# A transformer block on one core: VectorE copies the accumulator, maxima in another order, and two more blocks in seven products

## The chip, the core and the metric

The kernel runs on one core of a Trainium2 chip. The core has a matrix engine (TensorE, PE in the profile; PEld is its loading of weights), a vector engine (VectorE, DVE), an engine for functions (ScalarE, ACT), a general one (GpSimd, POOL), and a queue (SyncE, SP) that here only issues transfers (DMAs) between the chip's memory and the on-chip buffer, SBUF. TensorE writes to eight banks in a small memory of its own, PSUM; a bank holds 128 x 512 numbers of 32 bits. The metric is the device time of one execution, in microseconds (us).

## The reference

One block of a transformer in 32-bit floats: layer norm, attention of 32 heads of width 20, and a gated feed-forward part, each with its residual.

```python
B, S, D, H = 1, 2048, 640, 32
B, S, D, F = 1, 2048, 640, 1728
...
qkv = (x @ wqkv).reshape(B, S, 3, H, Dh)
scores = jnp.einsum("bhqd,bhkd->bhqk", q, k) * (Dh ** -0.5)
p = _softmax(scores, axis=-1)
o = jnp.einsum("bhqk,bhkd->bhqd", p, v)
return o.transpose(0, 2, 1, 3).reshape(B, S, D) @ wo
...
g = _silu(x @ w_gate)
u = x @ w_up
return (g * u) @ w_down
...
h = x + _A_ref(_layernorm(x, axis=-1), A_wqkv, A_wo)
h2 = h + _B_ref(_layernorm(h, axis=-1), B_w_gate, B_w_up, B_w_down)
```

## The kernel before

Each engine runs its own instructions in the order in which the program issues them; a manual schedule fixes that order, and tiles with few buffers make one engine wait for another. Numbers are kept exact by splitting a matrix into a high and a low part, so that one product takes three matmuls.

**Projections**, to about 350 us: queries, keys and values for all heads, and the first row maxima of the scores.

**Attention**, about 350 to 1450 us. The work is cut into 32 units: `u` counts groups of four heads times four chunks of 512 queries. A unit has 16 steps, `kt`, one for each 128 keys. In a step TensorE weighs the values of the step two before (`W`: `weigh`, four matmuls at once, one per head, into the tile `acc`, in records of L1319), and makes four products of scores (`s` for two heads, `S` for the other two, which lie in other rows of the array; L1309), each of which ScalarE turns into probabilities with one exponential (L1315). Between them stand three products whose row maxima VectorE takes for a later unit (`m` and `M`, L274 and L280; `next_max`). A string of letters in `ORDER` gives the order of one step; even and odd steps have one each. Scores rotate through four PSUM banks, maxima through three, and `acc` has the eighth: the next unit's first `W` can't begin until `acc` has been copied out. That copy is made in `row_sums` (L1329): it is issued in step 1 of the next unit, behind the last `W` of the unit, on ScalarE. Its transfers, a reciprocal in step 4 and a multiplication in step 9 follow.

When all maxima of a unit are there (`full`), VectorE joins them into one negative maximum per row (`max_all`, a reduction of 128 x 64), GpSimd splits it (`max_parts`), four steps later VectorE turns it (`max_turn`), and two steps after that it is loaded beside the queries (`max_load`).

In the same steps, one task per step, weights are prepared for the feed-forward part: `prepare_weights` leaves split blocks of the down weights in `d_d` (plain) and, for two blocks together, seven combinations in `j_d`.

**Feed-forward**, about 1500 us to the end. Tokens are taken in two halves (`pair` 0 and 1), and the 1728 hidden columns in 14 blocks `f`: the loop goes over 28 elements, `ELEMENTS`, in the order of blocks 13, 0, 1 to 12, once for each half. An element makes its gate and up products (`blocks`, L1492) in eight steps. After the products of a step, `step()` issues some down products that have become ready, taken from the queue `waiting` by `next_down`; how many per element is a number in `RATES`, spread evenly over its steps. VectorE adds the parts of gate and up (L1709), multiplies them to the hidden values `y` (L1713), and adds each down product to a sum.

A down group is 256 tokens (`tp` 0 to 3 in a half) against one block of the hidden columns (`plain`: four products of 3 matmuls, 320 columns wide, added to the result `h` by L1592) or two blocks (`seven`: seven products in place of eight, after Strassen and Winograd; three of them go to `h`, four to sums of their own, `own`, L1610). GpSimd and ScalarE prepare the operands, `yp`. After the last group in seven products the four sums are joined to `h` by eight additions (`put_together`, L1625), which are put in a list, `chores`, and issued on GpSimd, two in each `step()`. In the first half the blocks 2 to 11 go in seven products, in the second half the blocks 0 to 9; there blocks 10, 11, 12 and 13 are plain. Down products use four PSUM banks, gate and up four others. When the loop is over, the rest of `waiting` is issued, and the result of each 128 tokens is stored as soon as its last addition, that of block 12, is made (L1651).

Of the kernel before, what the change touches and what calls it, by code (L numbers as in the profile page):

```python
# [11 lines left out]
F32R = mybir.dt.float32r  # L12
# [26 lines left out]
GD = G * DH  # L39

ORDER = ("WsSmmSsM", "WSsMMsSm")


@with_exitstack
def tile_block(ctx: ExitStack, tc: tile.TileContext, x, wqkv, wo, wg, wu, wd, out):
# [15 lines left out]
    t_d = [dram.tile([P, 8 * CH], F32R, name=f"t_d{i}") for i in range(2)]  # L61
    w_d = [dram.tile([P, 8, 4 * P], F32R, name=f"w_d{f}") for f in range(NF)]
    d_d = {
        f: dram.tile([P, 2, 2 * HALF], F32R, name=f"d_d{f}") for f in (0, 1, *range(NF - 4, NF))
    }
    j_d = [dram.tile([P, 7, 2 * HALF], F32R, name=f"j_d{j}") for j in range((NF - 2) // 2)]
    h_d = dram.tile([2, P, TPC, D], F32, name="h_d")
# [216 lines left out]
    def max_all(u):  # L284

        ends[u] = stk.tile([P, G * TPC], F32, name="neg", tag="neg", bufs=2)
        nc.vector.tensor_reduce(  # L287
            ends[u], mxs[u].rearrange("p b h t k -> p (b h t) k"), axis=AX.X, op=ALU.max, negate=True
        )

    def max_parts(u):

        neg = ends[u]
        both = ends[u] = stk.tile([P, 2, G * TPC], F32R, name="neg2", bufs=2)
        nc.gpsimd.tensor_copy(both[:, 0], neg)  # L295
        nc.gpsimd.tensor_tensor(
            out=both[:, 1], in0=neg, in1=both[:, 0].bitcast(F32), op=ALU.subtract
        )

    def max_turn(u):  # L300

        turned = stk.tile([P, 2 * G * TPC], F32, name="turned", bufs=2)
        nc.vector.transpose(turned, ends.pop(u).bitcast(F32).rearrange("p i n -> p (i n)"))
        nc.sync.dma_start(m_d[u % 2], turned)

    def max_load(u):

        n = 2 * TPC
        rows = m_d[u % 2].rearrange("(q i r) c -> i r q c", q=4, i=2)
        for b in range(2):  # L310
            for i in range(2):
                row = b * ROW + NPART + i
                dst = queries[u][row : row + 1].bitcast(F32).rearrange("r j c -> r (j c)")
                nc.sync.dma_start(dst, rows[i, b * n : (b + 1) * n])

    def max_finish(u):

        m = (ps_one if u else ps_max)()[: G * TPC, :P]
        nc.tensor.transpose(m, ends.pop(u), ident)
        parts = stk.tile([G * TPC, 2, P], F32R, name="m2", tag="m2", bufs=1)  # L320
        split(m, parts[:, 0], parts[:, 1], nc.vector)
        for b in range(2):
            for i in range(2):
                row = b * ROW + NPART + i
                first = b * 2 * TPC
                nc.sync.dma_start(
                    queries[u][row : row + 1].bitcast(F32).rearrange(
                        "r j (t p) -> r (j t) p", t=TPC
                    ),
                    parts[first : first + 2 * TPC, i, :].bitcast(F32),  # L330
                )
# [994 lines left out]

    def row_sums(acc, *queues):
        o = pc.tile([P, CH], F32, name="o", bufs=2)
        nc.scalar.activation(o, acc, AF.Copy)  # L1329
        r = pc.tile([P, 16], F32, name="r")  # L1330
        for j in range(G):
            queues[j % len(queues)].dma_start(
                r[32 * j : 32 * j + 32, :],
                o[32 * j + DH : 32 * j + DH + 1, :].rearrange("r (p f) -> r p f", p=32),
            )
        return o, r
# [47 lines left out]
    for u in range(NU):  # L1384
# [9 lines left out]
        for kt in range(NT):  # L1394
            now[0] = u * NT + kt
            probs = [pp.tile([P, 2, CH], F32, name="probs") for _ in range(2)]
            heads = [[0, 2], [1, 3]]
            order = ORDER[now[0] % 2] if singles[0] or singles[1] else "WsSsS"
            for op in order:
                if op in "mM":  # L1400
                    next_max(int(op == "M"))
# [14 lines left out]
                        last_ring.fill()  # L1416
            todo.append((u, kt, probs))
            for v in full:
                max_all(v)
                if v in (1, NU - 1):  # L1420
                    later.setdefault(now[0] + 2, []).append(lambda v=v: max_finish(v))
                else:
                    max_parts(v)
                    later.setdefault(now[0] + 4, []).append(lambda v=v: max_turn(v))
                    later.setdefault(now[0] + 6, []).append(lambda v=v: max_load(v))
            full.clear()
            if kt == 0 and u + 3 < NU:
                load_queries(u + 3)
# [107 lines left out]

    def own(pair, f):

        return f >= NF - 4 if pair else f < 2 or f >= NF - 2

    SLOTS = ("A11", "A12", "A22", "S1", "S2", "S3", "S4")
    sums, chores, stored = {}, [], []
# [2 lines left out]
    class Group:  # L1545
# [68 lines left out]
        def put_together(self):  # L1614

            h = h_c[self.c]
            at = [h[:, self.t + i, k * HALF : (k + 1) * HALF] for i in range(2) for k in range(2)]
            one, six, seven, five = sums[self.tp]
            for out, x in (
                (at[0], one), (six, one), (at[1], six), (at[1], five), (seven, six),  # L1620
                (at[2], seven), (five, seven), (at[3], five),
            ):
                chores.append((
                    self.pair, self.tp,
                    lambda o=out, x=x: nc.gpsimd.tensor_tensor(out=o, in0=o, in1=x, op=ALU.add),  # L1625
                ))
# [33 lines left out]
    def next_down():  # L1660
        if not waiting:
            return
        g = waiting[0]
        prepare_some()
        f, i = g.steps.pop(0)
        f(i)
        if not g.steps:
            waiting.pop(0)
# [246 lines left out]
    def spread_over(n, steps, first=0):  # L1915
# [3 lines left out]
    RATES = {  # L1919
# [3 lines left out]
    }  # L1923
    again = []

# [78 lines left out]
        before = ys  # L2004
    while waiting:
        next_down()


_INS = ["A_x", "A_wqkv", "A_wo", "B_w_gate", "B_w_up", "B_w_down"]
# [26 lines left out]
```

## Time and profile before

| | |
|---|---|
| Median of 3 runs | 2009.06 us (2008.3 to 2011.39) |
| The profiled execution's own time | 2007.79 us |
| Its span in the trace | 2006.0 us |
| Busy: PE, DVE, ACT, POOL | 1997.4, 1602.9, 1434.6, 799.9 us |
| Exponentials (ACT L1315) | 2048, 613 ns each |
| Row maxima (DVE L280) | 1472, 684 ns each |
| Copies of the accumulator (ACT L1329) | 32, 629 ns each |

Times are counted from the start of the span; the execution is 1.8 us longer than its span. An engine takes the next instruction before the last one has ended, so the distance from one start to the next is less than the duration of one: it is called the pitch below. A busy PE is not PE at its peak, since the ends of matmuls are modelled: whether it lost time is read from the distances between starts.

### The profile page before, as it was taken

Reading aid. Unit: us, or ns where it says so; the run is one execution under the profiler, and the core shown is the slowest. Engines: PE = TensorE matmul, PEld = TensorE weight load, DVE = VectorE, ACT = ScalarE, POOL = GpSimd, SP = SyncE. Lnnn points to the kernel's source line nnn. Section 1 sums busy time; section 2 is a strip of 40 time slices with the busy share of each in tenths; the row PEclk is TensorE's granted clock in tenths of the full one; section 3 lists DMA queues with packets and bytes.
Section 4 is the critical chain, followed back from the end, with each engine's and each line's share of the span. In section 5 each row is a group of like instructions: output and inputs, shape, how many; then the busy total and the mean of one; then the engine's idle time right before and its main releaser. Section 6 shows DMA issues by size and latency. Waiting matters only on the chain.

```text
span 2006.0 us, 40039 instructions
## 1 busy us (share of the span) xinstructions
PE 1997.4 (100%) x14346; PEld 1246.5 (62%) x14346; DVE 1602.9 (80%) x2806; ACT 1434.6 (72%) x2811; POOL 799.9 (40%) x1206
## 2 busy tenths in 40 slices
PE   9999999999999999999999999999999999999999
PEld 8999995333333333333333333345598888888888
DVE  5778778898898888988988888886387766676677
ACT  4777778999999999999999999987633222212221
POOL 7564423344343443443500020011156444854555
PEclk9999999999999999999999999999999999999999
DMA  7887573442634534435412132221158654974542
GB/s 250 263 260 260 182 216 83 129 145 92 188 107 136 159 126 144 160 117 181 153 50 78 28 90 55 81 63 61 50 193 300 229 178 162 357 265 159 205 151 94
DMA packets 201541, 310.98 MB, mean 155 GB/s; under 512 B 55960, under 2 KB 89816, under 8 KB 200320
## 3 DMA queue, kind: packets, MB, share of 16 engines
q1 hardware_dynamic: 194752, 284.83, 43.5%
q0 software_dynamic: 6496, 23.60, 4.0%
q8 instruction: 114, 1.87, 0.4%
q14 instruction: 83, 0.68, 0.1%
q10 hardware_dynamic: 96, 0.00, 0.0%
HBM read 208.73 MB, written 99.32 MB: 154 GB/s over the span
## 4 chain that ended last, share of the span: by engine, by line
PE 99%; DVE 0%; ACT 0%; issue 0%; POOL 0%; POOLq 0%; DVEq 0%; ACTq 0%
PE acc L1319 25%; PE ps_a L1492 17%; PE ps_one L1309 16%; PE ps_max L274 13%; PE ps_one L647 10%; PE ps_b L1587 9%; PE ps_max L239 3%; PE ps_max L1037 2%; PE ps_b L1037 2%; PE ps_two L809 0%; PE ps_two L700 0%; PE ps_max L1072 0%; ACT ps_max L251 0%; PE ps_a L1858 0%; PE ps_max L573 0%
## 5 line engine op out<-in xcount | busy, mean ns | idle before, releaser
L1315 ACT ACTIVATE probs<-ps_one 128x512 f32<-128x512 f32 x2048 | 1055.9, 613 | 55.4 <-PE ps_one L1309 29.8
L280 DVE TENSOR_REDUCE mx<-ps_max 128x1 f32<-128x512 f32 x1472 | 924.9, 684 | 106.2 <-PE ps_one L1309 77.6
L1309 PE MATMUL ps_one<-q_stk,k_stk 62*128 62x512 f32 x2048 | 579.7, 448 | 0.3 <-ACT probs L1315 0.3
L1319 PE MATMUL acc<-probs,v_stk 128*32 128x512 f32 x4096 | 546.3, 604 | 0.0
L1309 PEld LDWEIGHTS ps_one<-q_stk,k_stk 62*128 62x128 f32 x2048 | 247.5, 184 | 444.7 <-ACT probs L1315 424.9
L274 PE MATMUL ps_max<-k_stk,q_stk 60*128 60x512 f32 x1472 | 373.5, 426 | 0.1
L274 PEld LDWEIGHTS ps_max<-k_stk,q_stk 60*128 60x128 f32 x1472 | 272.6, 186 | 26.7 <-DVE mx L280 1.3
L1709 DVE TENSOR_TENSOR tmp<-ps_a,tmp 128x512 f32<-128x512 f32 x208 | 141.2, 689 | 121.0 <-PE ps_a L1492 93.0
L261 DVE TENSOR_REDUCE mx<-ps_max 128x2 f32<-128x512 f32 x288 | 180.7, 684 | 60.2 <-PE ps_max L239 55.7
L1319 PEld LDWEIGHTS acc<-probs,v_stk 128*32 128x32 f32 x4096 | 80.9, 108 | 180.0 <-issue 167.8
L251 ACT ACTIVATE ps_max<-ps_max 128x512 f32<-128x512 f32 x288 | 151.8, 583 | 39.6 <-PE ps_max L239 38.2
L1587 PE MATMUL ps_b<-halves,yp 128*128 128x320 f32 x1032 | 178.7, 308 | 0.2 <-DVE h L1592 0.2
L1587 PEld LDWEIGHTS ps_b<-halves,yp 128*128 128x128 f32 x1032 | 165.2, 188 | 16.0 <-DVE h L1592 0.5
L1492 PE MATMUL ps_a<-t,units 128*128 128x512 f32 x624 | 162.5, 396 | 0.0
L1354 POOL TENSOR_TENSOR o<-o,rb 128x512 f32<-128x512 f32 x31 | 39.9, 1288 | 269.3 <-DMA q_stk<-m_d 146.5
L90 POOL TENSOR_TENSOR yp<-y,yp 128x256 fp32r<-128x256 f32 x96 | 60.4, 629 | 186.9 <-ACT yp L89 179.0
L1492 PE MATMUL ps_a<-z,units 128*128 128x512 f32 x516 | 133.9, 394 | 0.0
L1492 PEld LDWEIGHTS ps_a<-t,units 128*128 128x128 f32 x624 | 112.6, 188 | 18.5
L295 POOL CAST neg<-neg 128x16 fp32r<-128x16 f32 x30 | 5.9, 198 | 281.2 <-DVE neg L287 281.2
L1592 DVE TENSOR_TENSOR h<-ps_b,h 128x320 f32<-128x320 f32 x248 | 109.8, 480 | 5.8 <-PE ps_b L1587 4.3
L647 PE MATMUL ps_one<-z_hi,w_lo 64*128 64x512 f32 x380 | 111.8, 392 | 0.0
L647 PE MATMUL ps_one<-z_hi,w_hi 64*128 64x512 f32 x380 | 111.5, 393 | 0.0
(220 smaller groups left out, 2748.4 us busy)
## 6 DMA issues: line engine op xcount, KB each, us to landing
units<-w_d SPq DMA_DIRECT2D x186, 256.0 KB
w_d<-stage SPq DMA_DIRECT2D x106, 256.0 KB
halves<-j_d SPq DMA_DIRECT2D x70, 320.0 KB
j_d<-stage SPq DMA_DIRECT2D x42, 320.0 KB
raw<-k_d SPq DMA_DIRECT2D x64, 160.0 KB
k_stk<-k_d SPq DMA_DIRECT2D x64, 160.0 KB
q_stk<-q_d SPq DMA_DIRECT2D x64, 160.0 KB
raw<-q_d SPq DMA_DIRECT2D x54, 160.0 KB
```

What stands on the lines that cost most here:

```text
L251: nc.scalar.activation(ps, ps, AF.Relu)
L261: nc.vector.tensor_reduce(mx[:, b, :, t, kc], ps.rearrange("p (j n) -> p j n", j=2), axis=AX.X, op=ALU.max,)
L274: nc.tensor.matmul(ps, queries[u][rows, pair, t * P : (t + 1) * P], keys[u // NC][rows, pair, kc * CH : (kc + 1) * CH], start=True, stop=True,
L280: nc.vector.tensor_reduce(mxs[u][:, b, pair, t, kc : kc + 1], ps, axis=AX.X, op=ALU.max)
L647: nc.tensor.matmul(ps, a[rows], b[rows], start=(i == n == 0), stop=(i == 1 and n == last), skip_group_check=True,)
L1309: nc.tensor.matmul(ps, keys[u // NC][rows, p, kt * P : (kt + 1) * P], queries[u][rows, p, :], start=True, stop=True,)
L1315: nc.scalar.activation(probs[p][:, b, :], ps, AF.Exp, scale=scale)
L1319: nc.tensor.matmul(acc[32 * j : 32 * j + 32, :], values[u // NC][:, kt, j * VW : j * VW + 32], probs[j // 2][:, j % 2, :], start=(kt == 0) ...
L1492: nc.tensor.matmul(ps.rearrange("p (t n) -> p t n", t=TPC), w[k][:, i], z[k][:, :, j], start=(first and m == 0), stop=(last and m == len(n ...
L1587: nc.tensor.matmul(ps, a, b, start=(n == 0), stop=(n == len(pairs) - 1))
L1592: nc.vector.tensor_tensor(out=h, in0=ps, in1=h, op=ALU.add)
L1709: add = lambda out, ps, x: nc.vector.tensor_tensor(out=out, in0=ps, in1=x, op=ALU.add)
```

## The change

It has four parts. The copy of `acc` in `row_sums` goes from ScalarE to VectorE, in all units but the last. The first five steps of each unit but the first take their order from a new table, `BEGIN`. Where the maxima of a unit become complete in step 15, they are joined four steps later, and turned and loaded four steps later too. In the second half of the feed-forward part, blocks 10 and 11 go through the seven products; the joining of the sums therefore comes after them, just ahead of block 12. For the last two groups of tokens (`tp` 2 and 3) its eight additions are made at once on VectorE, and not put into the list for GpSimd. `RATES` of the last three elements are 16, 15 and 30 in place of 18, 22 and 26, and in the rest of `waiting` one of the list's additions is issued after each product.

```diff
+BEGIN = (
+    "WmSmsSMs", "WsSmSsMM", "WSsMMsmS", "WsMSmsSm", "WmSmsSsM",
+)
...
-        f: dram.tile([P, 2, 2 * HALF], F32R, name=f"d_d{f}") for f in (0, 1, *range(NF - 4, NF))
+        f: dram.tile([P, 2, 2 * HALF], F32R, name=f"d_d{f}") for f in (0, 1, *range(NF - 2, NF))
...
-        nc.scalar.activation(o, acc, AF.Copy)
+        if len(queues) == 1:
+            nc.vector.tensor_copy(o, acc)
+        else:
+            nc.scalar.activation(o, acc, AF.Copy)
...
-            order = ORDER[now[0] % 2] if singles[0] or singles[1] else "WsSsS"
+            order = BEGIN[kt] if u and kt < len(BEGIN) else ORDER[kt % 2]
+            if not (singles[0] or singles[1]):
+                order = "WsSsS"
...
-                max_all(v)
+                at = now[0]
                 if v in (1, NU - 1):
-                    later.setdefault(now[0] + 2, []).append(lambda v=v: max_finish(v))
+                    max_all(v)
+                    later.setdefault(at + 2, []).append(lambda v=v: max_finish(v))
                 else:
-                    max_parts(v)
-                    later.setdefault(now[0] + 4, []).append(lambda v=v: max_turn(v))
-                    later.setdefault(now[0] + 6, []).append(lambda v=v: max_load(v))
+                    if kt == NT - 1:
+                        at += 4
+                        later.setdefault(at, []).append(lambda v=v: (max_all(v), max_parts(v)))
+                    else:
+                        max_all(v)
+                        max_parts(v)
+                    later.setdefault(at + 4, []).append(lambda v=v: max_turn(v))
+                    later.setdefault(at + 6, []).append(lambda v=v: max_load(v))
...
-        return f >= NF - 4 if pair else f < 2 or f >= NF - 2
+        return f >= NF - 2 if pair else f < 2 or f >= NF - 2
...
+                if (self.pair, self.tp // 2) == (1, 1):
+                    nc.vector.tensor_tensor(out=out, in0=out, in1=x, op=ALU.add)
+                    continue
...
-        25: (18, 0), 26: (22, 0), 27: (26, 0),
+        25: (16, 0), 26: (15, 0), 27: (30, 0),
...
     while waiting:
         next_down()
+        if chores:
+            chores.pop(0)[2]()
```

On VectorE, at the start of a unit whose maxima became complete in step 15, before the change: `neg` is the joining, `turned` the turning, and each `mx` a row maximum of 128 x 512.

```order
L287 TENSOR_REDUCE neg<-mx_9492 128x16
L280 TENSOR_REDUCE mx_10182<-ps_max 128x1 x9
L303 STREAM_TRANSPOSE turned<-neg_10163 128x32
L280 TENSOR_REDUCE mx_10182<-ps_max 128x1 x6
L1340 RECIPROCAL r<-r 128x16
```

The same place after it:

```order
L283 TENSOR_REDUCE mx_10169<-ps_max 128x1 x3
L1333 COPY o<-acc 128x512
L283 TENSOR_REDUCE mx_10169<-ps_max 128x1 x6
L290 TENSOR_REDUCE neg<-mx_9490 128x16
L283 TENSOR_REDUCE mx_10169<-ps_max 128x1 x6
L1346 RECIPROCAL r<-r 128x16
L283 TENSOR_REDUCE mx_10169<-ps_max 128x1 x6
L306 STREAM_TRANSPOSE turned<-neg_10271 128x32
```

The copy stands behind the three maxima of step 0 and ahead of those of step 1; the joining has gone from the unit's first place to behind the maxima of step 2.

On TensorE, steps 0 and 1 of a unit before the change, from the last `W` but one of the unit before (`acc`) to its last:

```order
L1319 MATMUL acc<-probs,v_stk_5637 32x512 x4
L1309 MATMUL ps_one<-q_stk,k_stk_125 128x512 x2
L274 MATMUL ps_max<-k_stk_125,q_stk 128x512 x2
L1309 MATMUL ps_one<-q_stk,k_stk_125 128x512 x2
L274 MATMUL ps_max<-k_stk_125,q_stk 128x512
L1319 MATMUL acc<-probs,v_stk_5637 32x512 x4
```

The same place after it, and the products behind the last `W`:

```order
L1322 MATMUL acc<-probs,v_stk_5635 32x512 x4
L277 MATMUL ps_max<-k_stk_123,q_stk 128x512
L1312 MATMUL ps_one<-q_stk,k_stk_123 128x512
L277 MATMUL ps_max<-k_stk_123,q_stk 128x512
L1312 MATMUL ps_one<-q_stk,k_stk_123 128x512 x2
L277 MATMUL ps_max<-k_stk_123,q_stk 128x512
L1312 MATMUL ps_one<-q_stk,k_stk_123 128x512
L1322 MATMUL acc<-probs,v_stk_5635 32x512 x4
L1312 MATMUL ps_one<-q_stk,k_stk_123 128x512 x2
L277 MATMUL ps_max<-k_stk_123,q_stk 128x512
L1312 MATMUL ps_one<-q_stk,k_stk_123 128x512 x2
L277 MATMUL ps_max<-k_stk_123,q_stk 128x512 x2
```

Step 0 now begins with a product for a maximum, and step 1 ends with two of them; each step has its four products of scores and three of maxima as before.

On VectorE, from the last hidden values `y` to the program's end, before the change (`h_5622` is the result of tokens `tp` 0 and 1, `h_5623` that of `tp` 2 and 3):

```order
L1709 TENSOR_TENSOR tmp<-ps_a,tmp 128x512
L1713 TENSOR_TENSOR y<-tmp 128x512
L1592 TENSOR_TENSOR h_5623<-ps_b,h_5623 128x320
L1592 TENSOR_TENSOR h_5622<-ps_b,h_5622 128x320 x8
L1592 TENSOR_TENSOR h_5623<-ps_b,h_5623 128x320 x8
```

The same place after it (`h_5620` and `h_5621` are the same two results):

```order
L1726 TENSOR_TENSOR tmp<-ps_a,tmp 128x512
L1730 TENSOR_TENSOR y<-tmp 128x512
L1606 TENSOR_TENSOR h_5621<-ps_b,h_5621 128x320 x2
L1638 TENSOR_TENSOR h_5621<-h_5621,own 128x320
L1638 TENSOR_TENSOR own<-own 128x320
L1638 TENSOR_TENSOR h_5621<-h_5621,own 128x320 x2
L1638 TENSOR_TENSOR own<-own 128x320
L1638 TENSOR_TENSOR h_5621<-h_5621,own 128x320
L1638 TENSOR_TENSOR own<-own 128x320
L1638 TENSOR_TENSOR h_5621<-h_5621,own 128x320
L1606 TENSOR_TENSOR h_5620<-ps_b,h_5620 128x320 x8
L1606 TENSOR_TENSOR h_5621<-ps_b,h_5621 128x320 x8
```

The eight joining additions of `tp` 3 (L1638) now stand between the last seven products and the sixteen additions of block 12; those of `tp` 2 stand in the same way two steps earlier.

## The prediction

> **What bounds the kernel now.** I read the page first, then the busy times by stage, then stretches of the timeline where the edits are.
>
> ```profile
> span 2006.0 us, 40039 instructions
> PE 1997.4 (100%) x14346; PEld 1246.5 (62%) x14346; DVE 1602.9 (80%) x2806; ACT 1434.6 (72%) x2811; POOL 799.9 (40%) x1206
> PE 99%; DVE 0%; ACT 0%; issue 0%; POOL 0%; POOLq 0%; DVEq 0%; ACTq 0%
> ```
>
> TensorE is busy all the time and alone makes up the chain that ended last. But ends of matmuls are modelled, so small waits are hidden in these figures. The windows (columns: stretch, its length, busy time of PE, PEld, DVE, ACT, POOL, then clock, DMA share, GB/s) show the neighbours:
>
> ```profile
> 600.00:700.00 100.00, 100.00 (x705) 39.31 (x703) 89.81 (x149) 97.68 (x192) 40.41 (x75) 1.00 0.49 148
> 1700.00:1800.00 100.00, 100.00 (x519) 87.22 (x518) 70.77 (x134) 20.25 (x43) 64.51 (x88) 1.00 0.88 314
> 1950.00:2006.00 56.00, 51.82 (x290) 46.51 (x288) 40.25 (x84) 8.60 (x19) 34.76 (x44) 1.00 0.27 93
> ```
>
> In attention ScalarE (97.7) and VectorE (89.8) are nearly full too, at full clock. The last 56 us are the only stretch in which PE is clearly idle. So the change can act in two places: at the units' starts, and at the end.
>
> **Part 1, the copy and the order.** TensorE's timeline at the start of a unit (steps 1 to 3): every `W`, the first products of step 1, and the last scores of step 2:
>
> ```profile
> 589.54 1.06 PE L1319 MATMUL acc<-probs,v_stk 128*32 128x512 f32 x8
> 590.54 0.50 PE L1309 MATMUL ps_one<-q_stk,k_stk 62*128 62x512 f32 x2
> 590.88 0.39 PE L274 MATMUL ps_max<-k_stk,q_stk 60*128 60x512 f32 x1
> ...
> 591.66 1.07 PE L1319 MATMUL acc<-probs,v_stk 128*32 128x512 f32 x8
> ...
> 593.03 0.49 PE L1309 MATMUL ps_one<-q_stk,k_stk 62*128 62x512 f32 x1
> ...
> 593.52 0.49 PE L1309 MATMUL ps_one<-q_stk,k_stk 62*128 62x512 f32 x1
> ...
> 593.95 1.07 PE L1319 MATMUL acc<-probs,v_stk 128*32 128x512 f32 x8
> ...
> 596.08 0.64 PE L1319 MATMUL acc<-probs,v_stk 128*32 128x512 f32 x4
> ```
>
> From `W` to `W` it is 2.12 us, then 2.29, then 2.13: step 2 of the unit is 0.16 late. ScalarE says why:
>
> ```profile
> 556.84 0.63 ACT L1329 ACTIVATE o<-acc 128x512 f32<-128x512 f32 x1
> ...
> 590.88 0.63 ACT L1329 ACTIVATE o<-acc 128x512 f32<-128x512 f32 x1
> 591.36 4.72 ACT L1315 ACTIVATE probs<-ps_one 128x512 f32<-128x512 f32 x9
> ```
>
> The copy takes one pitch of ScalarE (591.36 - 590.88 = 0.48), nine exponentials follow without a gap, and with the copy five pitches (2.4) fall into a step of 2.12; the four PSUM banks of the scores take up a part, and the fourth product of scores, at 593.52, waits for the rest. Without the copy four pitches (1.9) fit. From one copy to the next (556.84 to 590.88) it is 34.04, 0.12 more than 16 steps of 2.12. Of the 31 copies that move, 29 stand in units (1 to 29) with such steps; the last two hold the projections too: 29 x 0.16 = **4.6 us less**.
>
> What is late next? VectorE, which gets the copy:
>
> ```profile
> 591.30 1.89 DVE L280 TENSOR_REDUCE mx<-ps_max 128x1 f32<-128x512 f32 x3 [0.23 <-PE ps_max L274]
> L1608 DVE COPY own<-ps_b 128x320 f32<-128x320 f32 x32 | 14.2, 480 | 0.4 <-PE ps_b L1587 0.4
> L1592 DVE TENSOR_TENSOR h<-ps_b,h 128x320 f32<-128x320 f32 x248 | 109.8, 480 | 5.8 <-PE ps_b L1587 4.3 <-POOL h L1625 1.4
> ```
>
> Three maxima take 1.89, so their pitch is (1.89 - 0.69) / 2 = 0.60 with a last one of 0.69, and 0.23 to 0.3 of a step is free. A copy of 512 columns out of PSUM isn't there; the one of 320 lasts as long as an addition (480 ns), so I take that of a maximum: pitch 0.60. In the place where it stood it would cost 0.3 more than is free. The new order makes room: step 0 begins with a product for a maximum, a slot earlier than before (the first product of scores starts 1.00 behind `W`, 590.54 - 589.54, the first for a maximum 1.34), so its three maxima end about 1.2 into step 1, when the last `W` (1.06 long) has just ended. The copy then runs from 1.2 to 1.9; the next `W` can follow about 0.15 later (today's copy ends at 591.51, and `W` starts at 591.66), at 2.05, ahead of the 2.12 that it takes anyway. Behind it the maxima of step 1 start at 1.8 and end 1.5 into step 2, just as the third bank is wanted: cover is thin, under 0.1. If it is missed, each unit loses up to the 0.16 that it won, or more by a maximum's wait; bounds for this part are -6 (1.4 more, if the steps of 2.13 run at 2.12 too in some units) and +3, and I take -4.6, the row of the stall itself. The joinings moved by four steps (0.2 on VectorE) leave just the place in which step 0 needs it; they load a unit's maxima a unit ahead, so nothing waits. Seven preparing tasks that go were GpSimd's and SP's, and no row of the chain names them: nothing.
>
> **Part 2, the seven products.** Per 256 tokens two plain blocks are 8 x 3 matmuls and become 7 x 3: 12 matmuls less in all. Rows of the end of the program (PE's matmuls, then VectorE's and GpSimd's operations):
>
> ```profile
> 1854.40 1.55 PE L1492 MATMUL ps_a<-z,units 128*128 128x512 f32 x6
> 1990.08 1.28 DVE L1592 TENSOR_TENSOR h<-ps_b,h 128x320 f32<-128x320 f32 x3
> 1994.09 0.69 DVE L1709 TENSOR_TENSOR tmp<-ps_a,tmp 128x512 f32<-128x512 f32 x1
> 1994.88 0.69 DVE L1713 TENSOR_TENSOR y<-tmp 128x512 f32<-128x512 f32 x1
> 1995.49 7.07 DVE L1592 TENSOR_TENSOR h<-ps_b,h 128x320 f32<-128x320 f32 x17
> 1996.03 5.74 PEld L1587 LDWEIGHTS ps_b<-halves,yp 128*128 128x128 f32 x39 [0.48 <-DVE h L1592]
> 1996.03 6.01 PE L1587 MATMUL ps_b<-halves,yp 128*128 128x320 f32 x39 [0.22 <-DVE h L1592]
> 1996.19 0.73 POOL L90 TENSOR_TENSOR yp<-y,yp 128x256 fp32r<-128x256 f32 x1 [3.98 <-ACT yp L89]
> ```
>
> A down matmul has a pitch of (6.01 - 0.31) / 38 = 0.15 (0.31 is one's duration), a product of three 0.45; a 512-wide one (1.55 - 0.39) / 5 = 0.23. So 12 x 0.15 = 1.8 us less on TensorE. VectorE's addition of 320 columns has a pitch of (1.28 - 0.48) / 2 = 0.40; one that needs the result of the one before it waits longer: the sum at 1994.09 and the `y` made of it at 1994.88 are 0.79 apart, where 0.61 would do, so 0.18 is added. Of the eight joining additions four follow such a predecessor: 8 x 0.40 + 4 x 0.18 = 3.9 us per group, if nothing else holds them.
>
> Something does. `y<-tmp` reads two operands from SBUF, as the joining additions will:
>
> ```profile
> 1854.55 1.29 POOL L90 TENSOR_TENSOR yp<-tmp,yp 128x512 fp32r<-128x512 f32 x1 [0.32 <-ACT yp L89]
> 1855.03 1.36 DVE L1713 TENSOR_TENSOR y<-tmp 128x512 f32<-128x512 f32 x1 [0.61 <-ACT tmp L1753]
> 1726.58 2.16 POOL L1625 TENSOR_TENSOR h<-h,own 128x320 f32<-128x320 f32 x2
> 1728.69 0.88 POOL L1625 TENSOR_TENSOR own<-own 128x320 f32<-128x320 f32 x1
> L1713 DVE TENSOR_TENSOR y<-tmp 128x512 f32<-128x512 f32 x48 | 42.4, 884 | 10.3 <-ACT tmp L1753 6.4
> ```
>
> Begun while GpSimd works, it takes 1.36 in place of 0.69: it waited until 0.14 ahead of GpSimd's end at 1855.84. Its mean is 884 ns, not 690, while L1592, with one operand in PSUM, keeps to 480 with GpSimd at work. GpSimd pays too: two of its additions took 2.16 at 1726.58, where one alone is 0.88 (1728.69). So a joining addition on VectorE and an operation of GpSimd take turns: 0.88 - 0.14 + 0.34 (320 columns at the difference of the two pitches, 0.20 / 192) = 1.08 per pair; with a `yp` (0.73) 0.93.
>
> By the new order, what has GpSimd to do then? For `tp` 2: the `yp` of block 12, tokens 0 and 1, which become ready with the `y` just ahead, and behind them four of the sixteen joining additions of `tp` 0 and 1. The first `yp` is nearly done, so five operations take turns with eight: 0.1 + 0.34 + 0.93 + 4 x 1.08 + 2 additions left (1.0) = **6.7 us**. For `tp` 3: the `yp` of the last `y`, the last four joining additions, another `yp`: from the start of `y` two additions (1.4), then 0.5 + 0.34 + 4 x 1.08 + 0.93 + 1.0 = 7.1, together **8.5**.
>
> Now the sum, from the moment when TensorE has made the last of the seven products of `tp` 2. VectorE: 1.4 until the joining (the sum, `y` and additions queued ahead), 6.7, then to the start of the last `y` one addition, two sums of 512, four additions and the wait (0.4 + 0.6 + 1.6 + 0.6 + 0.2 = 3.4), 8.5, and the sixteen additions of block 12, 6.5 (TensorE has four banks ahead and goes on at 0.45). That is 26.5. TensorE alone would need 23 products and 12 wide matmuls, 23 x 0.45 + 12 x 0.23 = 13.1, and 0.6 to the end of the last addition: 13.7. The end comes 26.5 - 13.7 = 12.8 later than TensorE needs; today it comes 0.5 later (the wait of 0.48 at 1996.03). What is queued behind the waiting additions on VectorE is the emptying of PSUM, so TensorE waits. **Part 2: -1.8 + 12.8 - 0.5 = +10.5 us.** Bounds: without the turns both joinings take 3.9, 6.0 less in all, +4.5; were an addition from SBUF half as long (0.2) and free of all waits, two of 1.6 remain and the part comes to 0; up to +13 if GpSimd's list is later still. I keep to the turns, since the row is of the same kind of operation. The loads of the down weights are seven in place of four, a step ahead of use; the operands `yp` of the new groups are made by GpSimd while its list is empty: nothing.
>
> The whole rule of which the turns are a part stands in the Trainium skill, "SBUF — State Buffer", section "Who interferes with whom": a VectorE instruction with two SBUF inputs contends with a GpSimd instruction that reads SBUF, and the first holds the lock for its whole instruction. The rows agree that it is exclusive, but show it freed 0.14 early, and VectorE's hold as 0.34, not 0.48; by the rule's letter ten full turns would cost some 0.28 each, 2.8 us more: 2017.8, inside the range below.
>
> **Rivals.** The sums are made against the profiled execution, 2007.8; the median is 1.3 above it, and the same differences are put to it. *Forecast*: -4.6 + 10.5 = +5.9, **2015.0**, chance 0.46. *No turns*: GpSimd's list is empty or elsewhere when VectorE joins; -4.6 + 4.5, 2009.0. For it: the list's place in time is my estimate; against: its order. 0.20. *The copy stalls*: VectorE is late for `acc` or the third bank, so part 1 gives nothing or up to +3; with +10.5, 2019.6 to 2022.6. For it: a margin under 0.1; 0.14. *Joining is cheap*, the other side: VectorE's additions from SBUF at 0.2 and free of waits, with part 2 at 0: 2004.5; hidden altogether, -1.8 - 0.5 more, 2002.2. It decides if the two joinings take under some 4 us together; no row shows VectorE at that pace. 0.10. *More than the stall goes*: some units run steps of 2.13, and all might run at 2.12 without ScalarE's load: 4 less, 2011. 0.10.
>
> Measuring this kernel can tell about 0.2%, 4.0 us, from no change. Faster by more: most of the cheap joining and a little of the second: 0.10. Within: the second, most of the fifth, and the low end of the forecast: 0.36. Slower: 0.54. The range leaves out the cheapest joining and the worst of the stalls: 2005 to 2021.
>
> **What would show it.** In attention every distance from `W` to `W` 2.12 to 2.13, with no 2.29; the copy ending 1.9 behind the last `W`. At the end joining additions with durations up to 1.2, GpSimd's `h<-h,own` stretched to 1.2 beside them, waits of TensorE for `h` and `own` in the last 25 us, and some 27 us from the first joining's products to the last addition. The forecast is wrong if the joinings take 4 us each (no turns), or if a step of 2.3 is still there in each unit.

## The result, and the profile after

The changed kernel takes 2023.22 us (median of 5 runs, 2022.27 to 2024.24), the kernel before 2009.06 (5 runs beside them): a ratio of 1.0069, with an interval of 1.0058 to 1.0080. That is 14.2 us slower, where 5.9 was forecast, and outside the range. Ratios, here and below, are worked out from all runs but one, a disturbed run of e10 (2403.35 us at a granted clock of 0.75), and not from the medians, from which they differ a little. The profiled execution took 2022.75 us. From the page of the kernel after, its span, its busy times and the chain that ended last by engine:

```profile
span 2021.0 us, 39921 instructions
PE 1999.8 (99%) x14334; PEld 1250.3 (62%) x14334; DVE 1629.7 (81%) x2849; ACT 1426.9 (71%) x2784; POOL 792.0 (39%) x1202
PE 98%; DVE 2%; ACT 0%; issue 0%; POOL 0%; DVEq 0%; POOLq 0%; ACTq 0%
```

VectorE has two per cent of the chain now, 30 to 50 us by the rounded share; before it had none. ScalarE lost the copies and VectorE got them. TensorE is still in nearly all of the chain, so where the time went is read by stage. From the first `W` of the attention to the start of the last two it was 318.54 to 1443.77 before, 1125.2 us, and is 319.24 to 1443.18 now, 1123.9: **1.3 less, where 4.6 was forecast**. From there to the end of the span it was 562.2 and is 577.8: **15.6 more, where 10.5 was forecast**. The 0.7 ahead of the first `W` is within the 2.0 by which that place moves between the traces of this document, which share that code.

**Attention.** TensorE's timeline of the kernel after, at the start of a unit (the rows of `acc` are `W`s, the last of the unit before being that at 624.12; the others are products of scores and for maxima):

```profile
622.01 1.07 PE L1322 MATMUL acc<-probs,v_stk 128*32 128x512 f32 x8
...
624.12 1.06 PE L1322 MATMUL acc<-probs,v_stk 128*32 128x512 f32 x8
...
625.69 0.49 PE L1312 MATMUL ps_one<-q_stk,k_stk 62*128 62x512 f32 x1
625.70 0.73 PE L277 MATMUL ps_max<-k_stk,q_stk 60*128 60x512 f32 x2
626.36 1.07 PE L1322 MATMUL acc<-probs,v_stk 128*32 128x512 f32 x8
...
628.47 1.07 PE L1322 MATMUL acc<-probs,v_stk 128*32 128x512 f32 x8
```

The distances are 2.11, 2.24, 2.11: the step of 2.29 is gone, and another, of 2.21 to 2.24, stands one step ahead of its place in nearly every unit. Its weight loads (PEld) and VectorE's copy in the same kernel:

```profile
625.69 0.18 PEld L1312 LDWEIGHTS ps_one<-q_stk,k_stk 62*128 62x128 f32 x1 [0.28 <-ACT probs L1318]
625.70 0.29 PEld L277 LDWEIGHTS ps_max<-k_stk,q_stk 60*128 60x128 f32 x2
626.36 0.16 PEld L1322 LDWEIGHTS acc<-probs,v_stk 128*32 128x32 f32 x8 [0.37 <-DVE o L1333]
```

```profile
621.65 3.78 DVE L283 TENSOR_REDUCE mx<-ps_max 128x1 f32<-128x512 f32 x6 [0.24 <-PE ps_one L1312]
625.35 0.68 DVE L1333 COPY o<-acc 128x512 f32<-128x512 f32 x1
625.94 1.88 DVE L283 TENSOR_REDUCE mx<-ps_max 128x1 f32<-128x512 f32 x3
```

The copy runs from 625.35 to 626.03, and the next step's maxima follow it at once: VectorE was in time, as forecast (1.2 to 1.9 behind the last `W`). The load at 625.69 is that of the fourth product of scores in `"WsSmSsMM"`. It waits 0.28 for ScalarE to free a bank, and the loads of both `M` stand behind it. The last of them is made late, and `W` with it. The third row names the copy as what `W` waited for; the experiments say whether it was.

**The end.** VectorE's timeline of the kernel after, from the first joining (L1638) to the last addition, then GpSimd's and TensorE's:

```profile
1988.18 0.93 DVE L1638 TENSOR_TENSOR h<-h,own 128x320 f32<-128x320 f32 x1
1989.03 1.16 DVE L1638 TENSOR_TENSOR own<-own 128x320 f32<-128x320 f32 x1
...
1996.25 0.48 DVE L1624 TENSOR_TENSOR own<-ps_b,own 128x320 f32<-128x320 f32 x1
...
2000.06 0.69 DVE L1730 TENSOR_TENSOR y<-tmp 128x512 f32<-128x512 f32 x1
...
2008.40 1.68 DVE L1606 TENSOR_TENSOR h<-ps_b,h 128x320 f32<-128x320 f32 x4
2010.28 0.49 DVE L1606 TENSOR_TENSOR h<-ps_b,h 128x320 f32<-128x320 f32 x1 [0.20 <-PE ps_b L1601]
2011.08 0.49 DVE L1606 TENSOR_TENSOR h<-ps_b,h 128x320 f32<-128x320 f32 x1 [0.31 <-PE ps_b L1601]
...
2014.21 3.19 DVE L1606 TENSOR_TENSOR h<-ps_b,h 128x320 f32<-128x320 f32 x7 [0.31 <-PE ps_b L1601]
```

```profile
1988.72 1.13 POOL L1642 TENSOR_TENSOR own<-own 128x320 f32<-128x320 f32 x1
...
1994.99 2.05 POOL L1642 TENSOR_TENSOR h<-h,own 128x320 f32<-128x320 f32 x2
```

```profile
1996.78 1.17 PE L1601 MATMUL ps_b<-halves,yp 128*128 128x320 f32 x3 [6.07 <-DVE own L1624]
...
2009.04 7.84 PE L1601 MATMUL ps_b<-halves,yp 128*128 128x320 f32 x36 [6.53 <-DVE h L1606]
```

The first joining takes 1988.18 to 1996.25, 8.1 us, with additions of up to 1.16 beside GpSimd's of up to 1.13; the last `y` begins 3.8 later, the second joining ends 8.3 behind it, and the sixteen additions take 2008.40 to 2017.40, 9.0. TensorE waits 6.07 and 6.53. After the second wait VectorE's additions are 0.80 apart, and **now they wait for TensorE**: three matmuls in 0.80 are 0.267 each, not 0.15. The windows of the kernel after (PEclk is the third column from the right) show the granted clock:

```profile
1975.00:1985.00 10.00, 10.00 (x57) 9.01 (x56) 7.33 (x16) 2.16 (x5) 9.28 (x15) 1.00 0.00 0
1985.00:1995.00 10.00, 5.71 (x33) 4.96 (x31) 9.21 (x12) 0.86 (x3) 9.56 (x10) 0.94 0.01 2
1995.00:2005.00 10.00, 5.73 (x24) 5.17 (x24) 9.45 (x16) 1.47 (x3) 5.60 (x6) 0.72 0.00 0
...
2010.00:2015.00 5.00, 5.00 (x23) 5.00 (x23) 3.32 (x8) 0.00 (x0) 0.00 (x0) 0.58 0.68 262
```

It goes from 1.00 to a mean of 0.58, while PE looks 100% busy in the last row: its 23 matmuls fill 5 us because each takes longer.

### The profile page after: what moved, and what is told of

It reads as the page before. It is cut to its first block, busy times and chain, and to the rows that moved or that the text cites. A ratio compares the mean times of both kernels' runs of the same rounds, so it can differ in the third digit from the quotient of the medians.

```text
span 2021.0 us, 39921 instructions
## 1 busy us (share of the span) xinstructions
PE 1999.8 (99%) x14334; PEld 1250.3 (62%) x14334; DVE 1629.7 (81%) x2849; ACT 1426.9 (71%) x2784; POOL 792.0 (39%) x1202
## 4 chain that ended last, share of the span: by engine, by line
PE 98%; DVE 2%; ACT 0%; issue 0%; POOL 0%; DVEq 0%; POOLq 0%; ACTq 0%
PE acc L1322 25%; PE ps_a L1506 17%; PE ps_one L1312 15%; PE ps_max L277 13%; PE ps_one L650 10%; PE ps_b L1601 8%; PE ps_max L242 3%; PE ps_max L1040 2%; PE ps_b L1040 2%; PE ps_two L812 0%; DVE h L1638 0%; PE ps_two L703 0%; DVE own L1638 0%; PE ps_max L1075 0%; ACT ps_max L254 0%
## 5 line engine op out<-in xcount | busy, mean ns | idle before, releaser
L1312 PE MATMUL ps_one<-q_stk,k_stk 62*128 62x512 f32 x2048 | 572.6, 444 | 0.2 <-ACT probs L1318 0.2
L1312 PEld LDWEIGHTS ps_one<-q_stk,k_stk 62*128 62x128 f32 x2048 | 262.3, 184 | 396.6 <-ACT probs L1318 375.2
L277 PE MATMUL ps_max<-k_stk,q_stk 60*128 60x512 f32 x1472 | 401.5, 429 | 0.1
L277 PEld LDWEIGHTS ps_max<-k_stk,q_stk 60*128 60x128 f32 x1472 | 263.6, 186 | 69.8 <-DVE mx L283 49.8
L92 ACT ACTIVATE yp<-tmp 128x512 fp32r<-128x512 f32 x44 | 27.8, 632 | 117.8 <-POOL tmp L1594 117.8
```

What stands on the lines that cost most here:

```text
L277: nc.tensor.matmul(ps, queries[u][rows, pair, t * P : (t + 1) * P], keys[u // NC][rows, pair, kc * CH : (kc + 1) * CH], start=True, stop=True,
L1312: nc.tensor.matmul(ps, keys[u // NC][rows, p, kt * P : (kt + 1) * P], queries[u][rows, p, :], start=True, stop=True,)
```

## The experiments

Medians are beside runs of the kernel before on the same chip; the ratio is to those.

| Kernel | Median, us | Before, us | Ratio, interval |
|---|---|---|---|
| e1: part 1 alone | 2007.70 | 2008.63 | 1.0000 (0.9991 to 1.0009) |
| e2: part 2 alone | 2024.46 | 2008.63 | 1.0077 (1.0063 to 1.0091) |
| e3: part 1, one letter moved | 2005.84 | 2008.63 | 0.9985 (0.9977 to 0.9994) |
| e7: part 1, old order | 2009.68 | 2009.21 | 1.0003 (0.9994 to 1.0011) |
| e8: e3, copy on ScalarE | 2009.88 | 2009.21 | 1.0006 (0.9997 to 1.0015) |
| e4: after, all joinings on VectorE | 2023.42 | 2008.63 | 1.0074 (1.0060 to 1.0087) |
| e5: after, no additions in GpSimd's list | 2016.35 | 2009.21 | 1.0034 (1.0021 to 1.0048) |
| e6: after, TensorE kept busy | 2021.29 | 2009.21 | 1.0059 (1.0045 to 1.0073) |
| e9: after, no joining | 2006.23 | 2008.78 | 0.9992 (0.9983 to 1.0001) |
| e10: after, all joinings on GpSimd | 2021.35 | 2008.78 | 1.0064 (1.0050 to 1.0078) |

### e1 and e2: each part alone

e1 has the new attention with the feed-forward part of before, e2 the reverse.

```diff
 e1, against the kernel after:
-        return f >= NF - 2 if pair else f < 2 or f >= NF - 2
+        return f >= NF - 4 if pair else f < 2 or f >= NF - 2
...
-                if (self.pair, self.tp // 2) == (1, 1):
-                    nc.vector.tensor_tensor(out=out, in0=out, in1=x, op=ALU.add)
-                    continue
...
 e2, against the kernel after:
...
-            nc.vector.tensor_copy(o, acc)
...
+        nc.scalar.activation(o, acc, AF.Copy)
-            order = BEGIN[kt] if u and kt < len(BEGIN) else ORDER[kt % 2]
...
+            order = ORDER[now[0] % 2] if singles[0] or singles[1] else "WsSsS"
```

> The changed attention (copy on VectorE, new order, later joinings) with the feed-forward part of before. In the changed kernel's trace every unit still has one late step, 2.23 from W to W in place of 2.29, now that of step 1. Theory: part 1 is worth 29 x 0.05 = 1.5 us, so about 2007.6, 0.1% faster than before, and everything else comes from part 2. Rival: the two parts hurt each other (part 1 alone would give its 4.6 us, or cost something): 2004.5, or above 2010.

> The attention of before with the changed feed-forward part (blocks 10 and 11 in seven products, joining of tokens 2 and 3 on VectorE, the new rates). Theory: all of the loss is here: 15 to 16 us over before, 2024 to 2025, with the two joinings at 8.1 and 6.9 us and the clock below 1.0 in the last 25 us. Rival: half of the loss or more belongs to attention's edits: under 2018.

Part 1 alone makes no difference that can be measured (1.0000); its late step of 2.17 to 2.23 is there without part 2. Part 2 alone gives 1.0077, the whole loss. No sign is seen that the parts act on each other: together they gave 1.0069 (1.0058 to 1.0080).

### e3, e7, e8: which edit of part 1 does what

e3 is e1 with one letter moved: the fourth product of scores of step 1 goes behind the products for maxima.

```diff
-    "WmSmsSMs", "WsSmSsMM", "WSsMMsmS", "WsMSmsSm", "WmSmsSsM",
+    "WmSmsSMs", "WsSmSMMs", "WSsMMsmS", "WsMSmsSm", "WmSmsSsM",
```

> As the run with the changed attention alone, but the fourth product of scores in step 1 stands behind both products for maxima (the step's order is WsSmSMMs in place of WsSmSsMM). Theory: in the changed kernel that product waits for its PSUM bank until ScalarE has ended the fourth exponential of step 0, and the weights of the two products for maxima queue behind it; moved back, every distance from W to W is 2.12 to 2.13 and part 1 gives its 4.6 us: about 2004.5. Rival: the late step comes from VectorE (the copy ends too late for acc, or the third bank of the maxima isn't free): the distance of 2.23 stays, 2007.6.

TensorE's timeline of e3 at the same unit, and then its weight load for `W`:

```profile
623.49 1.06 PE L1322 MATMUL acc<-probs,v_stk 128*32 128x512 f32 x8
...
625.05 0.39 PE L277 MATMUL ps_max<-k_stk,q_stk 60*128 60x512 f32 x1
625.05 0.44 PE L1312 MATMUL ps_one<-q_stk,k_stk 62*128 62x512 f32 x1
625.28 0.39 PE L277 MATMUL ps_max<-k_stk,q_stk 60*128 60x512 f32 x1
625.61 1.07 PE L1322 MATMUL acc<-probs,v_stk 128*32 128x512 f32 x8
```

```profile
625.61 0.16 PEld L1322 LDWEIGHTS acc<-probs,v_stk 128*32 128x32 f32 x8 [0.37 <-DVE o L1333]
```

The step is 2.12 long, and the attention, between the same two places as above, takes 1121.1 us, 4.1 less than before. With a ratio of 0.9985 (0.9977 to 0.9994) **e3 beats both kernels**, if by little. In both kernels `W` starts 0.32 to 0.33 us behind the last product for a maximum (626.04 in the kernel after, 625.28 here), and it is that product which came late. VectorE copies in the same place in its order in both. In the kernel after the copy ended 0.33 ahead of `W`, while in e7 (below) a `W` starts 0.05 behind the copy's end, at 627.70; so the copy was not what made the step late. The wait is labelled just as there, with the same 0.37: the label says only which of the conditions came last, not that it cost anything.

e7 leaves `BEGIN` out (copy on VectorE, `ORDER` everywhere); e8 has the order of e3 and the copy on ScalarE.

```diff
 e7, against e1:
-            order = BEGIN[kt] if u and kt < len(BEGIN) else ORDER[kt % 2]
+            order = ORDER[kt % 2]
 e8, against e3:
-        if len(queues) == 1:
-            nc.vector.tensor_copy(o, acc)
-        else:
-            nc.scalar.activation(o, acc, AF.Copy)
+        nc.scalar.activation(o, acc, AF.Copy)
```

> The changed attention with the copy on VectorE and the later joinings, but the old order of scores and maxima in all steps; the feed-forward part of before. Theory: with three maxima and the copy VectorE has 2.4 us of work in a step of 2.12 and no early maximum, so the copy ends some 0.25 later and the next unit's first W waits for acc: a step of 2.3 to 2.4 per unit, 2008 to 2011. Rival (VectorE has enough slack, and the order does nothing): all steps 2.12 to 2.13, 2005 to 2006.

> The order of the run with the fourth score last, and the later joinings, but the copy on ScalarE as before; the feed-forward part of before. Theory: it is the copy's place in ScalarE's queue that makes step 2 late, whatever the order: a step of 2.27 to 2.30 per unit stays, 2008 to 2009.5. Rival (the order alone heals it): all steps 2.12 to 2.13, 2005 to 2006.

The `W`s of e8 at the start of a unit, TensorE's timeline:

```profile
624.07 1.07 PE L1322 MATMUL acc<-probs,v_stk 128*32 128x512 f32 x8
...
626.19 1.06 PE L1322 MATMUL acc<-probs,v_stk 128*32 128x512 f32 x8
...
628.51 1.06 PE L1322 MATMUL acc<-probs,v_stk 128*32 128x512 f32 x8
```

With the copy on ScalarE the step of 2.32 is back, in the best order (626.19 to 628.51): the copy in ScalarE's queue makes that step. With the old order and the copy on VectorE (e7) two steps of a unit are late, 2.17 and 2.22, and not one of 2.3 to 2.4 as was expected; together they lose about what the old stall lost, and the ratio is 1.0003. So the place of the copy and the order with the moved letter are worth something only together. The later joinings stayed in all of these and were not tried apart.

### e5, e4, e9: what the joinings cost

e5 leaves out GpSimd's sixteen joining additions of tokens 0 and 1 (part of the result), and nothing on VectorE.

```diff
+                if self.pair == 1:
+                    continue
                 chores.append((
```

> The changed kernel without the sixteen joining additions of GpSimd for tokens 0 and 1 of the second half: this leaves out part of the result of those tokens. VectorE's own additions are all there. Theory: in the changed kernel two thirds of the 8.1 and 6.9 us of the joinings are turns with GpSimd; without its list only the operand splits of block 12 are left to take turns with, so the joinings take 4 to 5.5 us, and the time falls by 5 to 8 us against the changed kernel: 2015 to 2018. Rival (VectorE's additions are slow by themselves): joinings stay over 6.5 us and the time within 2 us of 2023.

VectorE's timeline of e5, the first joining and what follows it:

```profile
1989.33 0.50 DVE L1638 TENSOR_TENSOR h<-h,own 128x320 f32<-128x320 f32 x1
1989.76 1.02 DVE L1638 TENSOR_TENSOR own<-own 128x320 f32<-128x320 f32 x1
...
1992.67 0.48 DVE L1638 TENSOR_TENSOR own<-own 128x320 f32<-128x320 f32 x1
...
1993.60 0.48 DVE L1624 TENSOR_TENSOR own<-ps_b,own 128x320 f32<-128x320 f32 x1
```

The same eight additions take 4.3 us (1989.33 to 1993.60) in place of 8.1, the second joining 4.5 in place of 6.9. One is 0.48 long where GpSimd is quiet, and 1.02 where it makes a `yp`. The turns are shown: without GpSimd's list the program is 6.9 us faster (2016.35 to 2023.22; the ratios say 7.0), and still slower than before. In the traces 6.2 of it are in the two joinings and 0.8 in the sixteen additions, which take 8.2 here.

e4 takes the turns away in another way: all four joinings of the second half are made on VectorE, the sixteen additions with them.

```diff
-                if (self.pair, self.tp // 2) == (1, 1):
+                if self.pair == 1:
```

> The changed kernel with the joining of all four groups of tokens in the second half on VectorE, so GpSimd has none of these additions. Theory (VectorE and GpSimd take turns at operands from SBUF): the joinings fall from 8.1 and 6.9 us to some 4 to 5, TensorE's waits with them to under 4 us each, the clock stays at 1.0, and though VectorE has 16 additions more (6.4 us, some of it in idle time of its own) the time falls by 3 to 9 us against the changed kernel: 2014 to 2020. Rival (the additions are slow on VectorE by themselves, because each waits for the one before): joinings stay at 7 us or more, and the 16 additions more cost 6 us or more: 2029 and above.

It gained nothing (1.0074), and neither number was met. The joinings became short, 4.3 to 5.5 us each (1995.92 to 2000.19 that of `tp` 2), but there are four of them on VectorE, and TensorE waits earlier and oftener, as its timeline shows:

```profile
1982.54 3.41 PE L1601 MATMUL ps_b<-halves,yp 128*128 128x320 f32 x12 [2.90 <-DVE own L1624]
...
2000.73 1.17 PE L1601 MATMUL ps_b<-halves,yp 128*128 128x320 f32 x3 [3.05 <-DVE own L1624]
...
2010.58 6.82 PE L1601 MATMUL ps_b<-halves,yp 128*128 128x320 f32 x36 [3.14 <-DVE h L1606]
```

Twelve matmuls last 3.41 us at 1982.54, where 1.92 is usual: the clock is down (0.50 from 1983 to 1986) behind a wait of 2.90 already.

e9 leaves out all 32 joining additions of the second half, and so a part of the result.

```diff
-                if (self.pair, self.tp // 2) == (1, 1):
-                    nc.vector.tensor_tensor(out=out, in0=out, in1=x, op=ALU.add)
+                if self.pair == 1:
                     continue
```

> The kernel after the change, without any of the joining additions of the second half (32 additions of 320 columns, on VectorE and in GpSimd's list): the four sums of the last group in seven products are not added to the result, so a part of the result is left out. Theory (everything that part 2 costs is the joining and what follows from it): TensorE then has 12 matmuls less and nothing in return, so the time is that of the kernel with only the changed attention (ratio 1.0000 to before) less some 1.8 us: ratio 0.9985 to 0.9996, and PE shows no wait over 1.5 us in the last 40 us. Rival (the seven products cost something beside the joining, in emptying their sums or preparing their operands): ratio 1.000 or above, with waits of PE for `own`, `yp` or a PSUM bank left in the last 60 us.

It came out at 0.9992 (0.9983 to 1.0001), in the theory's range; the interval just reaches the rival, but the trace has none of the waits that it asks for: the longest of PE in the last 40 us is 0.22, ahead of its last row:

```profile
1993.44 6.43 PE L1601 MATMUL ps_b<-halves,yp 128*128 128x320 f32 x42 [0.22 <-DVE h L1606]
```

From the start of the last two `W`s to the end its trace has 561.2 us, e1's 562.6: by these two the twelve matmuls saved are worth 1.4. The kernels with the feed-forward part of before (before, e1, e3, e7, e8) have 562.2 to 563.0 there, so it may be 1.0 to 1.8. Everything else that part 2 costs is the joining and what follows from it; the new `RATES` stand in e9 too, and cost nothing that shows.

### e6 and e10: the clock, and the other engine

e6 is the kernel after with 25 and 27 matmuls more, 512 wide, whose results nobody reads, put where TensorE waits.

```diff
+    def keep_going(n):
+        ps, z = bank(), z2_c[0]
+        for _ in range(n):
+            nc.tensor.matmul(ps, z[:, :P], z[:, CH : 2 * CH], start=True, stop=True)
...
+                if (e, n, j) == (2 * NF - 1, 6, 3):
+                    keep_going(25)
...
+        if rest_of_them == 2:
+            keep_going(27)
```

> The changed kernel with 25 and 27 extra matmuls of 128 x 512, whose results nobody reads, put where TensorE waits for VectorE during the two joinings (6.4 and 6.8 us; they take 5.8 and 6.3 at 0.23 each). Theory: the granted clock falls because TensorE stood idle for 6 us, and this doubles the pitch of the matmuls behind (0.267 in place of 0.147), which holds up the sixteen last additions; kept busy, the clock stays at 1.0, the pitch at 0.147, the last additions are 0.44 apart, and the time falls by 2 to 3.5 us: about 2020.5. Rival (the slow matmuls have another cause, such as PSUM in VectorE's hands): the pitch stays at 0.267 and the time is the same or up to 1 us longer.

Windows of e6, and the last row of VectorE's timeline:

```profile
1985.00:1995.00 10.00, 10.00 (x53) 8.75 (x52) 9.60 (x13) 0.72 (x2) 9.77 (x10) 1.00 0.01 2
1995.00:2005.00 10.00, 8.70 (x45) 7.20 (x44) 9.83 (x16) 1.47 (x3) 5.97 (x7) 1.00 0.00 0
...
2010.00:2015.00 5.00, 3.87 (x27) 3.60 (x25) 4.40 (x11) 0.00 (x0) 0.00 (x0) 1.00 1.02 387
```

```profile
2007.72 6.68 DVE L1606 TENSOR_TENSOR h<-ps_b,h 128x320 f32<-128x320 f32 x16
```

The clock stays at 1.00, and the sixteen additions take 6.7 us, not 9.0, with the joinings as slow as they were (8.2 and 7.0). The clock also had a part in the stretch from the end of the first joining to the start of the last `y`: that is 3.4 here (1995.92 to 1999.29) and 3.8 in the kernel after, where VectorE waits 0.35 for TensorE in it. So the clock costs that kernel 2.7 us ahead of its last addition, which ends here at 2014.40 in place of 2017.40 (0.4 of that lies ahead of the first joining). The median is 1.9 lower, just under the 2 to 3.5 of the expectation; the intervals of the two ratios (1.0059 and 1.0069) overlap, so the gain of the whole program is likely, and not clear of the noise. Of the 3.0, 1.4 is lost again between the last addition and the end, which is 5.0 here and 3.6 in the kernel after. The stores of the result are still on their way then: their last transfer ends 3.2 behind the last addition in e6 (from 2016.5 on at a DMA share of 0.06), and 1.9 behind it in the kernel after. Why the last ones trail in e6 is left open.

e10 gives all 32 joining additions to GpSimd's list.

```diff
-                if (self.pair, self.tp // 2) == (1, 1):
-                    nc.vector.tensor_tensor(out=out, in0=out, in1=x, op=ALU.add)
-                    continue
                 chores.append((
```

> The kernel after the change, with all 32 joining additions of the second half in GpSimd's list (none on VectorE). Theory (the loss is VectorE standing in turns with its PSUM emptying queued behind): VectorE is free, TensorE runs on, and GpSimd has 32 additions of 0.88 us (28 us) and four operand splits of 0.73 (3 us) from about 1973 on, so it ends near 2004 and the last additions of block 12, which touch the same result, follow a few us later: span 2006 to 2012, ratio 0.9995 to 1.003, far below the 1.0069 of the change. Rival (GpSimd's list becomes the bound instead, since additions for the same result alternate between the two engines and each waits for the other): last addition on GpSimd later than 2012, ratio 1.004 or above.

The rival held, at 1.0064. TensorE's timeline of e10, two rows of VectorE's, and one of the windows:

```profile
1998.60 0.71 PE L1601 MATMUL ps_b<-halves,yp 128*128 128x320 f32 x3 [1.44 <-DVE h L1606]
2000.36 1.17 PE L1601 MATMUL ps_b<-halves,yp 128*128 128x320 f32 x3 [1.05 <-DVE h L1606]
```

```profile
2004.02 0.49 DVE L1606 TENSOR_TENSOR h<-ps_b,h 128x320 f32<-128x320 f32 x1 [2.21 <-POOL h L1639]
2005.79 0.49 DVE L1606 TENSOR_TENSOR h<-ps_b,h 128x320 f32<-128x320 f32 x1 [1.27 <-POOL h L1639]
```

```profile
2000.00:2010.00 10.00, 5.82 (x15) 3.84 (x15) 2.76 (x6) 0.00 (x0) 9.61 (x12) 0.50 0.25 98
```

VectorE now waits for GpSimd before each addition to `h`, up to 2.21, since the list's additions go to the same result; the last addition of the list ends at 2014.5. Of the places tried for the joining none makes part 2 pay: it would have to cost less than the 1.0 to 1.8 us that e9 wins.

## Why the prediction was wrong in size

The direction and the places were right: attention a little shorter, the loss in the last 40 us, made by joinings on VectorE. Between the forecast (+5.9) and the result (+15.0 in the span of the trace, 14.2 in the medians) lie these steps.

**"I take -4.6, the row of the stall itself."** The stall went, as e8 shows by bringing it back. What failed is the next question, "What is late next? VectorE, which gets the copy". VectorE's cover was judged rightly: the copy ended 1.9 behind the last `W`, and the maxima followed in time. What came next was ScalarE again: `"WsSmSsMM"` puts a product of scores, which waits for its fourth exponential, ahead of two products that needn't wait, and their weight loads go in the order of the program. 0.11 in 29 units is 3.2 of the 4.6; 1.3 were measured. The order's rows stood in the text ahead of the prediction; they were read for VectorE alone. With the letter moved e3 has 4.1. The rival "the copy stalls" had a step late near that place and nearly the price (up to 0.16), but the wrong engine; that its time, 2019.6 to 2022.6, lay nearest to the result was luck, since part 1 lost nothing and the miss at the end made it up.

**"The sixteen additions of block 12, 6.5 (TensorE has four banks ahead and goes on at 0.45)."** This is the largest miss at the end of the program: 9.0. The forecast had TensorE wait through both joinings and then go on at the pitch of a TensorE that never waits. The clock was 0.58 there, a product of three took 0.80, and TensorE held up VectorE. e6 takes that away and gives 6.7.

That waits lower the clock stands in the Trainium skill, "TensorE: Matmul & The Clock Gate", section "Why this matters for your kernels", which asks for no gaps over some 3 us between bursts of matmuls. The waits of 6.07 and 6.53 agree. But in e4 the pitch is down behind a wait of 2.90, in e5 behind one of 2.28 (the clock is 0.55 from 1994 to 1995), and in e10 behind waits of 1.44 and 1.05 with three matmuls between them. This speaks for a sum of idle time and not only one long gap; no run varied the waits alone.

**"6.7" and "8.5", the two joinings.** Measured: 8.1, and 8.3 from the last `y` (6.9 of it the joining, forecast 7.1). The turns hold (e5), and so does their price: eight additions in 8.07 us are 1.01 each, where a pair was put at 1.08 with a GpSimd addition and 0.93 with a `yp`. The first sum was too small because GpSimd's list was later than its place by the order: five operations were counted to take turns with, and from 1988.2 to 1996.3 there were nine. This was named as a bound ("if GpSimd's list is later still").

On the same rows the rule weighed in the prediction (the Trainium skill, "SBUF — State Buffer", section "Who interferes with whom") is right that one engine stops the other, while turns of full length (0.88 + 0.48 with an addition, 0.73 + 0.48 with a `yp`) would have made eight additions, two of them beside a `yp`, last 10.6. Measured were 8.1, and that decides.

**"Then to the start of the last `y` 3.4"** was 3.8, by the clock again, since it is 3.4 in e6. **"12 x 0.15 = 1.8 us less"** was 1.4 by e9 against e1, and with 1.0 to 1.8 over all such pairs it is not shown to be wrong.

The terms together: attention +3.3, the additions +2.5, the first joining +1.4, the second -0.2, the 3.4 and 1.8 +0.8, from 5.9 to 13.7. The span says 15.0; of the 1.3 that is left, 0.7 lies ahead of the first `W`, where the program is the same. The other 0.6 is open.

## What to carry to other kernels

When a stall is removed, read the new order for every engine that the following instructions wait for, and put what waits for the busiest of them behind what needn't wait: one letter was worth 2 us here (the medians of e1 and e3). Before additions are moved onto an engine that empties PSUM, ask what TensorE does meanwhile; a wait of a few us costs itself and then, through the clock, something more (2.7 us here). Next to a working GpSimd an addition with two SBUF operands on VectorE took about twice as long (1.01 us, 0.5 without), and even with GpSimd's list gone eight of them took 4.3 us, which 12 matmuls saved (1.4 us) can't pay for.

## What the runs showed of the hardware that was not expected

52 unread matmuls in two waits kept the clock at 1.00 and made the sixteen additions behind them 2.3 us faster (e6). The clock changes in steps between 1.0 and 0.5, and in the kernel after it does so at 1993.7, 2000.5, 2007.4 and 2014.2, each 6.8 us behind the last (in e5 3.4 or 6.8): it fell 3.0 us into the first long wait and 4.9 us into the second. The granted clock was 0.50 over ten us in e10, although no wait of TensorE there was over 1.5 us; three matmuls of the same shape took 0.71 us at 1998.60 and 1.17 at 2000.36. Weight loads for products that needn't wait stood behind one that did (625.69 and 625.70 in the kernel after). And the profile named the copy as what `W` waited for both where the step was late and where it was not.
